# A fused attention and MLP kernel: four-sum products, casts in quarters, output banks redistributed, stores moved to ScalarE

## The chip, the cores and the metric

The kernel runs on one core of one Trainium2 chip. The metric is device time in microseconds (us). Engines are TensorE (PE), VectorE (DVE), ScalarE (ACT), GpSimd (POOL) and the synchronisation engine (SP), which in the kernel before issues every transfer. A ratio is the mean time of one kernel's fast runs over the mean of the other's fast runs in the same rounds, so it is not quite the ratio of the medians that are quoted beside it. A run is called slow when it is over 1.5% above the fastest of the same kernel; such runs count in no ratio, but the medians quoted include them.

## The reference, cut to what matters

```python
def sm_attn(qq, kk, vv):                       # softmax attention, scale 1/8
    ...
p_packed = sm_attn(p, k, v)                    # 32 packed rows per head attend to 576 keys
out = sm_attn(q, p_packed, p_packed)           # 576 queries attend to the 32 rows
x = out.transpose(0, 2, 1, 3).reshape(4608, 512)
h = x @ w_in                                   # 512 -> 2048
g = h * (1.0 / (1.0 + np.exp(-beta * h)))
return g @ w_out                               # 2048 -> 512
```

Eight batches, eight heads, 576 tokens of 64 per head. In a batch, 512 tokens are two units of output work of 256 tokens; the remaining 64 tokens of four batches together make one more unit. That is 18 units. The last product, `g @ w_out`, is done for nearly all units as a 2x2 block product with seven instead of eight block multiplications.

## The kernel before: the parts that the change and the argument touch

The program is ordered by a planner in the kernel itself. It holds tasks with an estimated duration, dependencies and a rank; it simulates the engines and emits each engine's instructions in the order that it finds. The real chip then keeps that order on each engine, whatever the real times are.

```python
LAND_US = 2.0                                  # assumed from the end of an issue to the landing
...
def plan_loads(self, b):                       # per batch: k, v, q; fp32 staging, two buffers
    ...
    m0 = m1 = self.task(None, "SP", 3.1, lambda m=main: m(0, 8), last, turn)
    ...
    c0 = self.task(("cast", b, x, 0), "POOL", 1.95, lambda f=piece: f(0, 8, "POOL"), [m0] + old, rank + 3)
...
        if b >= PE_BATCHES:                    # from batch 2 on kT and qT are made by a transfer
            d = self.task(("tr", b, x, 0), "SP", 3.0, lambda x=x: transpose_dma(x), ...)
...
self.op = pool("op", 2)                        # two output staging buffers o_sb
self.ps_h = pool("ps_h", 2, space=PSUM)
self.ps_o = pool("ps_o", 3, space=PSUM)
self.ps_a = pool("ps_a", 3, space=PSUM)
...
def sums(i):                                   # three VectorE instructions, up to 128 x 2048
    if i == 0: nc.vector.tensor_tensor(S[:, 0:2], g[:, 0:2], g[:, 2:4], ALU.add)
    elif i == 1: nc.vector.tensor_tensor(S[:, 2], g[:, 0], g[:, 3], ALU.add)
    else: nc.vector.tensor_tensor(g[:, 1:3], g[:, 1:3], g[:, 0:4:3], ALU.subtract)
...
# five takes of 512 columns from PSUM to o_sb; the first waits for the store of the unit before last
t = self.task(("take", unit, i), "DVE" if i else "ACT", 0.7 if i else 0.64, ...
              + ([("store", back)] if back and i == 0 else []), ...)
self.task(("store", unit), "SP", 1.5, lambda: self.store(unit), [t], -10)
```

(Dots and shortened calls are cuts.) The whole kernel:

The softmax here doesn't subtract the row's maximum and nothing guards it: scores larger than these inputs give would overflow.

## Time and profile before

| | before |
|---|---|
| median of three runs | 261.63 us |
| span of the profiled run | 259.1 us |
| granted TensorE clock, mean | 0.998 |
| TensorE, VectorE, ScalarE, GpSimd busy | 241.7, 199.2, 176.1, 63.4 us |

The page gives a busy time per engine, tenths of it over 40 slices, and groups of instructions; the trace behind it gives each instruction with what ended the idle time before it. On TensorE the printed end of a matmul is modelled, so its work has to be counted from the distances between starts. The prediction below shows the lines and reads them.

### The profile page before, as it was taken

The page shows a single profiled execution, that of the slowest core. Times are in us where ns is not written, and L with a number is a line of the kernel's source. Part 1 is how long each engine was busy: PE and PEld are TensorE (multiplying, and loading weights), DVE is VectorE, ACT ScalarE, POOL GpSimd, SP SyncE. Part 2 cuts the span into 40 slices and gives each one's busy share as a digit, 9 for nine tenths or more (in the row PEclk, how much of TensorE's full clock was granted, in tenths as well). Part 3 has the DMA queues.
Part 4 walks back from the last instruction along what each step waited for, and adds up shares of the span by engine and source line. Part 5 has one row for each costly group of instructions (what it writes and reads, how often), then busy time and mean ns, then how long its engine had stood idle before and what let it go on. Part 6 is the DMA issues. An engine that isn't in the chain of part 4 may idle for free.

```text
span 259.1 us, 6793 instructions
## 1 busy us (share of the span) xinstructions
PE 241.7 (93%) x2897; PEld 193.8 (75%) x2897; DVE 199.2 (77%) x288; ACT 176.1 (68%) x308; POOL 63.4 (24%) x58
## 2 busy tenths in 40 slices
PE   4899689899989999998999999999999999999990
PEld 4897576566554878886778877877889778889880
DVE  6476766887985987796888968979996688665771
ACT  1153579867877878879786987886898768765000
POOL 4320433151440741342315231600900000000000
PEclk9999999999999999999999999999999999999999
DMA  7999999997998998996998999989660102201113
GB/s 225 352 320 268 280 325 384 348 330 183 288 199 237 292 246 235 212 333 148 265 251 263 143 318 291 205 227 272 174 172 7 79 0 83 82 27 60 81 81 81
DMA packets 73471, 54.18 MB, mean 209 GB/s; under 512 B 42065, under 2 KB 66657, under 8 KB 73441
## 3 DMA queue, kind: packets, MB, share of 16 engines
q1 hardware_dynamic: 73440, 53.76, 75.2%
q8 instruction: 22, 0.36, 0.6%
q14 instruction: 9, 0.07, 0.1%
HBM read 37.23 MB, written 9.44 MB: 180 GB/s over the span
## 4 chain that ended last, share of the span: by engine, by line
PE 56%; DMA 20%; SPq 10%; ACT 4%; issue 3%; POOL 3%; DVE 2%; POOLq 0%
PE o_ps L194 31%; PE h_ps L194 14%; DMA k<-in_k_dram 9%; SPq L336 5%; DMA v<-in_v_dram 4%; PE w_ps L194 3%; DMA qT<-q_bf 3%; SPq L250 2%; PE hr_ps L194 2%; DMA q32r<-in_q_dram 2%; DMA v32r<-in_v_dram 2%; PE z_ps L194 2%; PE s_ps L194 1%; SPq L242 1%; ACT g_main L639 1%
## 5 line engine op out<-in xcount | busy, mean ns | idle before, releaser
L639 ACT ACTIVATE g_main<-h_ps 128x512 bf16<-128x512 f32 x128 | 71.1, 596 | 29.5 <-PE h_ps L194 28.6
L194 PE MATMUL h_ps<-A2T,W_bf 128*128 128x256 bf16 x512 | 70.2, 273 | 0.6 <-ACT g_main L639 0.6
L194 PEld LDWEIGHTS <-W_bf 128*128 128x128 bf16 x768 | 57.1, 98 | 12.7 <-issue 4.7
L194 PE MATMUL o_ps<-w_mix,g_main 128*128 128x256 bf16 x448 | 59.5, 273 | 0.0
L194 PEld LDWEIGHTS <-g_main 128*128 128x128 bf16 x512 | 48.2, 98 | 12.5 <-issue 2.9
L600 DVE TENSOR_TENSOR W_bf<-w_ps,beta_bc 128x512 bf16<-128x512 f32 x64 | 41.5, 682 | 5.7 <-PE w_ps L194 5.2
L194 PEld LDWEIGHTS <-g_sums 128*128 128x128 bf16 x384 | 36.4, 98 | 5.5 <-issue 1.4
L209 ACT ACT_TABLE_LOAD x28 | 35.9, 1283 | 1.2 <-PEq L1067 0.7
L194 PE MATMUL o_ps<-w_out_bf,g_sums 128*128 128x256 bf16 x256 | 33.9, 273 | 0.0
L707 DVE TENSOR_TENSOR g_sums<-g_main 128x2048 bf16<-128x2048 bf16 x14 | 21.8, 1555 | 4.8 <-ACT g_main L639 4.8
L194 PE MATMUL warm_ps<-identr 128*128 128x128 bf16 x256 | 21.9, 237 | 3.7 <-DVE bones L858 3.7
L276 POOL CAST q_bf<-q 128x2048 bf16<-128x2048 f32 (+1 forms) x7 | 14.6, 2081 | 33.5 <-DMA q<-in_q_dram 19.9
L194 PEld LDWEIGHTS <-identr 128*128 128x128 bf16 x256 | 18.0, 108 | 5.5 <-DVE bones L858 3.7
L276 POOL CAST v_bf<-v 128x2048 bf16<-128x2048 f32 (+1 forms) x7 | 13.4, 1912 | 26.2 <-PE h_ps L194 9.8
L774 DVE TENSOR_TENSOR o_sb<-o_sb,o_ps 128x512 f32<-128x512 f32 x16 | 11.0, 685 | 10.0 <-ACT g_main L639 2.5
L541 DVE TENSOR_TENSOR A2T<-E2T,rz 128x512 bf16<-128x512 bf16 (+1 forms) x24 | 13.6, 587 | 5.5 <-ACT rz L536 5.5
L276 POOL CAST k_bf<-k 128x2048 bf16<-128x2048 f32 (+1 forms) x7 | 12.4, 1771 | 21.4 <-DMA k<-in_k_dram 10.4
L711 DVE TENSOR_TENSOR g_main<-g_main 128x2048 bf16<-128x2048 bf16 x14 | 17.4, 1244 | 0.0
L194 PE MATMUL o_ps<-w_mix,g_sums 128*128 128x256 bf16 x128 | 17.3, 273 | 0.0
L194 PE MATMUL o_ps<-w_out_bf,g_main 128*128 128x512 bf16 x64 | 17.0, 380 | 0.0
L772 ACT COPY o_sb<-o_ps 128x512 f32<-128x512 f32 x16 | 9.4, 588 | 10.3 <-PE o_ps L194 10.2
L194 PEld LDWEIGHTS <-pp 64*32 64x32 bf16 x384 | 6.0, 88 | 13.5 <-issue 10.9
(86 smaller groups left out, 296.5 us busy)
## 6 DMA issues: line engine op xcount, KB each, us to landing
out_dram<-o_sb SPq DMA_DIRECT2D x16, 512.0 KB, 3.9
k<-in_k_dram SPq DMA_DIRECT2D x7, 1024.0 KB, 8.5
v<-in_v_dram SPq DMA_DIRECT2D x7, 1024.0 KB, 6.8
q<-in_q_dram SPq DMA_DIRECT2D x7, 1024.0 KB, 6.7
w_in<-in_moe_w_in_dram SPq DMA_DIRECT2D x4, 1024.0 KB, 9.4
w_out<-in_moe_w_out_dram SPq DMA_DIRECT2D x4, 1024.0 KB, 12.4
k<-in_k_dram SPq DMA_DIRECT2D x2, 512.0 KB, 5.4
k32r<-in_k_dram SPq DMA_DIRECT2D x16, 64.0 KB, 5.2
```

Of the source, the lines that this page charges most:

```text
L194: return self.nc.tensor.matmul(out, lhsT, rhs, start=start, stop=stop, tile_position=pos, skip_group_check=True)
L209: self.nc.scalar.preload_act_table_set(SETS[mode])
L250: nc.sync.dma_start(t[64 * g : 64 * g + 64, :].rearrange("p (h d) -> p h d", h=4), src[b, 4 * g : 4 * g + 4, SM:S, :].rearrange("h p d -> ...
L276: self.copy[engine](self.t[b, x][:, 0:2048].rearrange("p (t h d) -> p h t d", t=4, h=8)[:, h], self.t[b, x, "32"][:].rearrange("p (h t d) ...
L336: nc.sync.dma_start_transpose(t[:], st[b, x][:])
L541: nc.vector.tensor_tensor(part(st[b, "A2"], i), part(st[b, "E2"], i), part(st[b, "rz2"], i), ALU.mult)
L600: nc.vector.tensor_tensor(st[b, "W"][:, r, cols], st[b, "w", m][:], self.beta_bc[:, cols], ALU.mult)
L639: nc.scalar.activation(st[b, v, "g"][:, :, f, :], st[b, "h", v, f][:].rearrange("p (q n) -> p q n", q=4), AF.Silu)
L707: nc.vector.tensor_tensor(st[*unit, "S"][:, 0:2], g[:, 0:2], g[:, 2:4], ALU.add)
L711: nc.vector.tensor_tensor(g[:, 1:3], g[:, 1:3], g[:, 0:4:3], ALU.subtract)
L772: nc.scalar.copy(middle, st[*unit, "C"][:])
L774: nc.vector.tensor_tensor(ends, middle.rearrange("p (h n) -> p h n", h=2)[:, ::-1], halves(st[*unit, "D"]), ALU.subtract)
```

## The change

Its intent is to take work from VectorE and to shorten both the waits behind it and the tail. The seven products are rewritten with four sums of 128x1024 on each side (one form of instruction instead of three), and accumulate in place in two PSUM banks; takes are 256 columns wide. GpSimd casts in pieces of a quarter, so that no piece holds VectorE up for long. The softmax normalisation of the packed rows moves into pointer operands of later instructions. The PSUM banks go from h 2, o 3, att 3 to h 3, o 2, att 3. Every task gets a rank offset of its own. All stores but the last two units' are issued from ScalarE.

```diff
+STORE_US = 5.0
+STORE = 'ACT'
+RINGS = {'h': 3, 'o': 2, 'att': 3}
+OFFSETS = {0: -0.9, 1: -8.9, 2: -158.2, ...}          # 1,130 entries, cut
 def add(self, engine, us, fn, deps=(), rank=0, ...):
+    rank += OFFSETS.get(len(self.tasks), 0)
...
-    self.copy[engine](bf[:, h], f32[:, h])             # 128 x 2048
+    m = 2 if engine == "POOL" else n
+    for j in range(0, n, m):
+        self.copy[engine](to[:, j : j + m], of[:, j : j + m])   # 128 x 512
...
-    d = self.task(("tr", b, x, 0), "SP", 3.0, ...)
+    d = self.task(("tr", b, x, 0), "SP", 3.8, ...)
...
+    out, a, b, op = {0: (s[:, 0], a21, a22, ALU.add), 1: (s[:, 1], s[:, 0], a11, ALU.subtract),
+                     2: (s[:, 2], a12, s[:, 1], ALU.subtract), 3: (a21, a11, a21, ALU.subtract)}[i]
+    nc.vector.tensor_tensor(out, a, b, op)
...
+    steps = [(("g", 2), "B21", 1, True), (("g", 0), "B11", 0, True), (("S", 0), "T1", 1, True), (("S", 1), "T2", 0, False),
+             (("S", 2), "B22", 1, False), (("g", 1), "T3", 0, False), (("g", 3), "T4", 0, False)]
...
-    nc.vector.tensor_tensor(W[:, r, cols], w_ps, self.beta_bc[:, cols], ALU.mult)
+    nc.vector.scalar_tensor_tensor(W[:, r, cols], w_ps, rz1[:, r : r + 1], self.beta_bc[:, cols], ALU.mult, ALU.mult)
...
-    self.task(("store", unit), "SP", 1.5, lambda: self.store(unit), [t], -10)
+    e = STORE if len(self.outs) < 17 else "SP"
+    self.task(("store", unit), e, us, lambda: self.store(unit, e), deps, -10)
```

(The order of the first loads, of the units of the last batch and many ranks change as well.)

## The prediction

> **What bounds the kernel now.** I read the page's busy tenths first, then the stretches of 20 us, then TensorE's timeline at the two ends, then the groups by line.
>
> ```profile
> PE   4899689899989999998999999999999999999990
> ...
> ACT  1153579867877878879786987886898768765000
> ...
> PEclk9999999999999999999999999999999999999999
> DMA  7999999997998998996998999989660102201113
> ```
> The clock is never throttled, so it is no part of the story. DMA is full until about 190 us, TensorE from about 60 us on. The stretches (TensorE, its weight loads, VectorE, ScalarE, GpSimd; then clock, DMA share, GB/s) say it more sharply:
>
> ```profile
> 20.00:40.00 20.00, 16.43 (x275) 13.36 (x273) 14.41 (x26) 11.64 (x23) 5.54 (x7) 1.00 1.02 296
> ...
> 60.00:80.00 20.00, 19.18 (x208) 11.49 (x206) 16.94 (x22) 14.78 (x26) 6.04 (x5) 1.00 0.93 224
> 80.00:100.00 20.00, 20.00 (x222) 15.06 (x219) 18.05 (x24) 16.52 (x30) 8.73 (x6) 1.00 1.00 251
> ...
> 160.00:180.00 20.00, 20.00 (x263) 16.25 (x261) 17.75 (x26) 15.21 (x26) 5.52 (x4) 1.00 0.99 249
> ...
> 220.00:240.00 20.00, 20.00 (x210) 18.03 (x208) 12.36 (x17) 12.82 (x23) 0.00 (x0) 1.00 0.14 55
> ```
> From 80 us TensorE is busy 20.00 of 20. But is it streaming, or are only modelled ends joined up? In its timeline the starts of consecutive pieces give the true spacing: eight 256-column matmuls take 0.87 us, 0.109 each; sixteen 64-column hr matmuls 0.47 us (0.029 each). Counting every matmul of 80 to 120 us at such spacings gives 39.9 of 40 us, of 160 to 200 and 200 to 240 us 40, of 120 to 160 us 38.8, of 47 to 80 us 29.9 of 33. The steady state is thus a full TensorE, and the full DMA there costs it about 1 us: one late transpose at 122 us. A faster VectorE buys nothing by itself.
>
> The start is different: TensorE runs fillers on warm_ps while it waits for loads.
>
> ```profile
> 46.13 0.41 PE L194 MATMUL w_ps<-w_in_bf,pp 64*32 64x512 bf16 x8
> 46.47 0.51 PE L194 MATMUL warm_ps<-identr 128*128 128x128 bf16 x6
> 46.91 0.39 PE L194 MATMUL w_ps<-w_in_bf,pp 64*32 64x512 bf16 x1
> 47.63 0.41 PE L194 MATMUL w_ps<-w_in_bf,pp 64*32 64x512 bf16 x7 [0.33 <-DVE W_bf L600]
> ...
> 75.76 0.41 PE L194 MATMUL s_ps<-qT,pp 64*32 64x512 bf16 x8 [0.79 <-DMA qT<-q_bf]
> ```
> The last filler ends at 47 us. After it the program has 488 h, 896 output (256 columns), 64 plain output (512 columns, 0.2175 each), 256 hr, 224 w and some 420 small matmuls: 53.1 + 97.5 + 13.9 + 7.5 + 12.3 + 16.0 = 200.3 us. TensorE ends at 253.1, so 206.1 us pass: 5.8 us are holes, 3.1 of them before 80 us. The tail is 6 us:
>
> ```profile
> 252.07 1.04 PE L194 MATMUL o_ps<-w_mix,g_sums 128*128 128x256 bf16 x8
> ...
> 253.15 0.69 DVE L782 TENSOR_TENSOR o_sb<-o_sb,o_ps 128x512 f32<-128x512 f32 x1 [0.19 <-PE o_ps L194]
> 253.87 2.46 SPq L809 DMA_DIRECT2D out_dram<-o_sb  x4
> ```
> One take, four issues that need 2.46 us, and the last landing at 259.1. So span = 47 (start) + 200.3 (work) + 5.8 (holes) + 6 (tail).
>
> **What the Trainium skill says.** "SBUF — State Buffer", section "SBUF: two separate sides": VectorE and GpSimd share a port pair as an exclusive lock for a whole instruction, and a VectorE operation with two SBUF inputs contends with a GpSimd operation that reads SBUF. This trace agrees (shortest, median and longest ns of the sums' two forms):
>
> ```profile
> L707 DVE TENSOR_TENSOR g_sums<-g_main x14: 1208/1224/2914, 71.8 to 236.4; 128x2048 bf16<-128x2048 bf16 x14
> ...
> L709 DVE TENSOR_TENSOR g_sums<-g_main x14: 676/782/2374, 74.4 to 237.5; 128x1024 bf16<-128x1024 bf16 x14
> ```
> and from the groups by line:
> ```profile
> L276 POOL CAST q_bf<-q 128x2048 bf16<-128x2048 f32 (+1 forms) x7 | 14.6, 2081 | 33.5 <-DMA q<-in_q_dram 19.9
> ```
> The longest sums exceed the shortest by 1.7 us, nearly one whole GpSimd cast. "VectorE: DVE Perf Modes", the section on the TRN2 errata, gives (N+151)/0.96 ns for an fp32 tensor_tensor: 691 ns at 512, and the output takes here show 685; so I estimate 0.42 us at 256. "ScalarE: Activation LUTs", "What ACT_TABLE_LOAD costs": each 128x1 pointer operand adds about 93 ns; nothing in this trace has one, so that stays an estimate. "DMA: Bandwidth & Descriptors", "Issuing engines are not separate DMA queues": issuing from another engine saves sequencer time only. The trace cannot show that yet, but the synchronisation queue waits 55.5 us in total in front of stores (14.3 the longest) and TensorE is still full.
>
> **The change part by part.**
>
> (a) TensorE's work. The built program of the changed kernel orders 254 fillers (256 before) and, behind the last, 480 h, 952 output, 32 plain, 256 hr, 208 w, 60 z1 and the small ones: 52.2 + 103.6 + 7.0 + 7.5 + 11.4 + 17.3 = 199.0 us. Both forms have seven products of 8 matmuls at 256 columns, so the new form saves no product. One unit less is plain: 32 x 0.2175 - 56 x 0.109 = -0.9 us in all. z1 becomes ten one-column matmuls (about 0.028 each by the 64-column spacing) for ten of 128 columns (0.40 us): -0.12 per batch, -0.7 in the six batches concerned. Eight h and 16 w matmuls moved ahead of the last filler (-1.8), transposes of q and scores moved behind it (+2.1). Sum: -1.3 us.
>
> (b) VectorE. Sums: 61.2 us now; 17 units x 4 x 0.68 = 46.2. Takes: 43.9 + 2.7 now; 102 x 0.42 + 2 x 0.69 = 44.2. The 128-column reciprocal (8 x 0.952 = 7.6) becomes 2 columns, about 0.16 each: 1.3. Normalising (16 x 0.287 = 4.6) becomes one copy, 8 x 0.42 = 3.4. Mixes 6.1 to 4 x 1.22 = 4.9. W_bf, 64 x 0.682 = 41.5, gets a pointer operand: I allow 46. Sum 167.6 to 146: VectorE falls from 199 to about 178 us busy. None of it lies on TensorE's path in the steady state, so its worth is slack.
>
> (c) ScalarE. Takes 16 x 0.588 to 17 x 0.38 (-3.0), 32 exponentials with a pointer scale (+3.0), 26 table loads for 28 (-2.6); 19 store issues at about 0.5 us join its queue. About even at 68% busy.
>
> (d) GpSimd's casts in quarters. The longest lock-out of a sum falls from some 1.7 us to about 0.5, for some 0.1 us more per piece on an engine that is 24% busy.
>
> (e) PSUM. Output now accumulates in two banks; a step may start only when the take of the preceding step on its bank is done. That take costs about 0.2 (as long as takes sit idle behind the last matmul in the trace) + 0.42 + 0.1 = 0.72 us. I laid TensorE's new order out at the spacings above: of 85 such waits, 81 have at least 0.87 us of other matmuls in between, three have 0.34 to 0.43, and the very last has none (a hole of 0.7 us). About a third have under 0.95: slack only if VectorE is free. The third h bank removes the small waits for g_main (0.2 us each around 50 us).
>
> (f) Loads. The last w_in stands behind 12.2 MB in both orders, so the fillers should end at the same time, 46 to 47 us. The last w_out comes after 16.5 MB instead of 17.7, some 4 us earlier at 300 GB/s: it loosens the stretch to 80 us, where 3.1 us of holes are.
>
> (g) Tail. The last unit is now one store instead of four: saves up to 1.9 us of issue; the take shrinks by 0.27. Tail 4.5 instead of 6, plus the hole of (e).
>
> Sum: 46.5 + 199.0 + 3.5 (holes) + 0.7 + 4.5 = 254.2 us of span. The medians lie 2.5 above the span now, so 256.7; I say 256.8. The holes are my choice: fewer late transposes (they are now planned later) and smaller lock-outs, against tighter takes.
>
> **Rivals.**
> 1. The take becomes the bound. If VectorE is 0.2 to 0.4 us late at a third of the 85 waits, 28 x 0.2 to 0.4 = 6 to 11 us of holes appear in place of 3.5: 259 to 264 us. For it: the 0.15 us of slack. Against it: VectorE is 20 us lighter, and most waits have over 1 us.
> 2. Nothing moves: the order is as full as before, and holes come back elsewhere, at a late DMA or ScalarE, which now also waits for takes before it issues stores. Then only (a) and (g) remain: 258 to 260.
> 3. The start shortens too, because q's first loads no longer wait for a staging buffer and less of the early queue stalls: fillers end at 43 to 44 us, and 252 to 254 is possible. Against it: DMA is already full from 6 us, and the fillers' number is unchanged.
>
> **Range and chances.** Without any hole the floor is about 46 + 199 + 5 + 2.5 = 252.5; with rival 1 in force 262. I put 80% on 253 to 261. Faster by over 2% means below 256.4, almost my centre: 0.43; within 2% 0.51; slower 0.06, as that would need 12 us of new holes.
>
> **What would show it.** Fillers end at 46 to 47 us; VectorE busy about 178 us; sums' longest near 1.2 us instead of 2.4 to 2.9; TensorE's holes after the fillers 3 to 4 us; from the last matmul to the end about 4.5 us. I am wrong if TensorE waits for VectorE's or ScalarE's takes at o_ps for over 5 us in all (rival 1), or if the fillers end 2 us away from 47.

## The result, and the profile after

The changed kernel is correct and slower: median 272.28 us of four runs (269.0 to 273.89, two of them slow), against 262.14 of four runs of the kernel before beside it. The ratio of fast runs is 1.0304, with a 95% interval of 1.0212 to 1.0397. The profiled run is a fast one: span 267.2 us, against 259.1.

The tenths of the changed kernel's page, to be laid beside those of before:

```profile
PE   4958769898994999999999799989999999999893
...
PEclk9999979999999799999999999999999999999999
```

TensorE's row now has a 4 in the slice from about 80 to 87 us and dents later; the clock's row has a 7 twice, in the slices from 33 and from 87 us, where the row of before has nothing but 9. The stretches (TensorE, its weight loads, VectorE, ScalarE, GpSimd; clock, DMA share, GB/s) say where:

```profile
80.00:100.00 20.00, 16.50 (x183) 12.45 (x182) 14.14 (x25) 12.35 (x24) 9.57 (x17) 0.91 1.03 231
...
140.00:160.00 20.00, 18.61 (x191) 15.69 (x189) 13.59 (x26) 15.85 (x30) 3.43 (x6) 1.00 0.99 213
```

TensorE, busy 20.00 of 20 in both of these stretches in the kernel before, is idle 3.5 us in the first, where its clock averages 0.91, and 1.4 us in the second. TensorE's timeline in the changed kernel (in brackets its idle time just before, and what ended it):

```profile
35.59 0.39 PE L296 MATMUL w_ps<-w_in_bf,pp 64*32 64x512 bf16 x2 [3.40 <-POOL w_in_bf L1095]
...
49.90 0.34 PE L296 MATMUL warm_ps<-identr 128*128 128x128 bf16 x3
...
86.99 0.41 PE L296 MATMUL s_ps<-qT,pp 64*32 64x512 bf16 x8 [3.50 <-DMA qT<-q_bf]
...
89.74 1.90 PE L296 MATMUL o_ps<-w_mix,g_sums 128*128 128x256 bf16 x8
91.56 0.25 PE L296 MATMUL s2r_ps<-qT,pp 64*32 64x64 bf16 x8
...
152.06 1.08 PE L296 MATMUL h_ps<-A2T,W_bf 128*128 128x256 bf16 x8 [1.39 <-ACT g_main L756]
```

The last filler starts at 49.90 and so ends near 50, 3 us later than before. The second scores of batch 2, which began at 75.76 us, begin at 86.99, after 3.5 us of waiting for the transposed q. Right behind that wait eight output matmuls take 91.56 - 89.74 = 1.82 us instead of 0.87: the clock has halved. With the same counting as in the prediction, 199.0 us of work follow the last filler, TensorE ends at 263.1, and 263.1 - 50 - 199.0 = 14 us are holes and slow clock, against 5.8 us. The tail is 4.1 us.

Why is qT late? The chain of what released what, in the changed kernel (start, duration, what):

```profile
69.50 4.21 DMA k<-in_k_dram
73.71 0.41 POOL q_bf L399
...
74.28 12.66 DMA qT<-q_bf
```

The transfer that transposes q took 12.66 us from its issue to its landing; in the kernel before it was issued at 70.98 and landed in time for the scores at 75.76, so at most 4.8 us. The synchronisation engine's queue in the changed kernel shows its neighbours:

```profile
69.50 0.55 SPq L358 DMA_DIRECT2D k<-in_k_dram  x1
...
73.74 0.38 SPq L358 DMA_DIRECT2D v<-in_v_dram  x1
74.28 6.92 SPq L453 DMA_TRANSPOSE qT<-q_bf  x1
```

Two loads of 1 MB each stand ahead of it, that of v directly, and its issue alone took 6.92 us. In the kernel before the load of v follows qT:

```profile
70.98 2.90 SPq L336 DMA_TRANSPOSE qT<-q_bf  x1
...
79.02 0.58 SPq L242 DMA_DIRECT2D v<-in_v_dram  x1
```

And the cast of q, which has to be done first, was itself slower. GpSimd's timeline of the changed kernel, then of the kernel before:

```profile
68.38 5.33 POOL L396 CAST q_bf<-q 128x512 bf16<-128x512 f32 x4
```
```profile
67.73 1.89 POOL L276 CAST q_bf<-q 128x2048 bf16<-128x2048 f32 x1 [4.24 <-DMA q<-in_q_dram]
```

Four quarters took 5.33 us where the whole took 1.89. The trace says where the time went: one by one they took 1.68, 1.60, 1.60 and 0.61 us, and each of the first three lay beside a w_mix difference on VectorE, of two operands in SBUF. The second and third of these, in VectorE's timeline:

```profile
69.84 1.29 DVE L1135 TENSOR_TENSOR w_mix<-w_out_bf 128x2048 bf16<-128x2048 bf16 x1
...
71.39 1.29 DVE L1135 TENSOR_TENSOR w_mix<-w_out_bf,w_mix 128x2048 bf16<-128x2048 bf16 x1
```

The median quarter takes 0.61 us, so four that are left alone take some 2.5. The sums, on the other hand, did what was hoped: the longest of the first form in the changed kernel is 1.15 us (before, 2.9 for a sum twice as large and 2.4 for one of the same size).

```profile
L837 DVE TENSOR_TENSOR g_sums<-g_main x15: 674/683/1154, 58.3 to 249.7; 128x1024 bf16<-128x1024 bf16 x15
```

The second clue is the 1.39 us wait for ScalarE at 152.06. ScalarE's timeline of the changed kernel, where ACTq is its queue issuing a transfer:

```profile
151.02 0.34 ACTq L922 DMA_DIRECT2D out_dram<-o_sb  x1
151.41 2.06 ACT L756 ACTIVATE g_main<-h_ps 128x512 bf16<-128x512 f32 x4 [2.68 <-DVE o_sb L886]
```

A store stood at the head of ScalarE's queue until 151.02, as the take that it stores was not done, and everything behind it stood too. (The release that the line names, the take, was the store's; g_main does not need it.)

### The profile page after: what moved, and what is told of

Read it like the earlier page. It is cut to its first block, busy times and chain, and to the rows that moved or that the text cites. A ratio compares the mean times of both kernels' runs of the same rounds, so it can differ in the third digit from the quotient of the medians.

```text
span 267.2 us, 6970 instructions
## 1 busy us (share of the span) xinstructions
PE 242.7 (91%) x2919; PEld 196.5 (74%) x2919; DVE 179.9 (67%) x335; ACT 171.1 (64%) x307; POOL 73.9 (28%) x119
## 4 chain that ended last, share of the span: by engine, by line
PE 63%; DMA 23%; SPq 4%; DVE 4%; POOL 2%; issue 1%; ACT 1%; ACTq 0%; POOLq 0%
PE o_ps L296 37%; PE h_ps L296 16%; DMA w_in<-in_moe_w_in_dram 6%; DMA qT<-q_bf 5%; DMA q<-in_q_dram 4%; DMA w_out<-in_moe_w_out_dram 4%; PE w_ps L296 3%; PE hr_ps L296 3%; SPq L366 3%; DMA v32r<-in_v_dram 2%; DMA k<-in_k_dram 2%; PE s_ps L296 1%; PE z_ps L296 1%; PE pp_ps L296 1%; DVE W_bf L717 1%
## 5 line engine op out<-in xcount | busy, mean ns | idle before, releaser
L717 DVE SCALAR_TENSOR_TENSOR W_bf<-w_ps,rz,beta_bc 128x512 bf16<-128x512 f32 x64 | 45.6, 744 | 5.9 <-PE w_ps L296 5.9
L884 DVE TENSOR_TENSOR o_sb<-o_sb,o_ps 128x256 f32<-128x256 f32 x51 | 21.3, 418 | 29.9 <-PE o_ps L296 26.0
L296 PE MATMUL o_ps<-w_out_bf,g_main 128*128 128x256 bf16 (+1 forms) x272 | 39.9, 285 | 1.1 <-DVE w_out_bf L1110 0.9
L296 PE MATMUL o_ps<-w_mix,g_sums 128*128 128x256 bf16 x272 | 37.5, 278 | 0.6 <-DVE o_sb L886 0.6
L296 PE MATMUL o_ps<-w_mix,g_main 128*128 128x256 bf16 x240 | 32.6, 273 | 0.5 <-DVE o_sb L884 0.5
L886 DVE COPY o_sb<-o_ps 128x256 f32<-128x256 f32 x51 | 21.3, 420 | 16.9 <-PE o_ps L296 16.4
L396 POOL CAST q_bf<-q 128x512 bf16<-128x512 f32 x26 | 19.8, 799 | 40.9 <-DMA q<-in_q_dram 40.9
L396 POOL CAST k_bf<-k 128x512 bf16<-128x512 f32 x26 | 17.6, 717 | 26.8 <-DMA kT<-k_bf 11.2
L396 POOL CAST v_bf<-v 128x512 bf16<-128x512 f32 x26 | 16.6, 678 | 10.3 <-PE pp_ps L296 3.9
L296 PE MATMUL o_ps<-w_out_bf,g_sums 128*128 128x256 bf16 x136 | 18.5, 273 | 0.1
```

The lines of the kernel that those rows point to most:

```text
L296: return self.nc.tensor.matmul(out, lhsT, rhs, start=start, stop=stop, tile_position=pos, skip_group_check=True)
L396: self.copy[engine](to[:, j : j + m], of[:, j : j + m])
L717: nc.vector.scalar_tensor_tensor(st[b, "W"][:, r, cols], st[b, "w", m][:], st[b, "rz1"][:, r : r + 1], self.beta_bc[:, cols], ALU.mult, AL ...
L884: nc.vector.tensor_tensor(o, o, ps, ALU.add)
L886: self.copy[engine](o, ps)
```

## The experiments

After the result I held three theories. **A**, late arrivals: the new program makes things arrive late (qT behind v, loads and casts, a store that blocks ScalarE, an output buffer whose store has not landed), and the new form is as good as predicted. **B**, rival 1 of the prediction: takes on two output banks are too tight. **C**: a lower clock is the cause and not a consequence. All seventeen kernels gave correct results. The medians of the kernel before were 261.64 (whole casts, qT first, stores from the synchronisation engine, twice the fillers), 262.49 (third buffer, no offsets, quarters alone, three undone), 264.04 (stores from ScalarE in the kernel before, the filled hole, four undone), 263.15 (quarters, halves, split tail), 261.94 (v ahead again, two buffers again) and 262.06 (stores from ScalarE again). Six of the eleven runs of the kernel before count as slow, only because one run took 259.44; with all eleven counted three ratios, 1.0354, 1.0291 and 1.0075, would be 1.0285, 1.0225 and 1.0008.

### One suspect undone at a time

Casts whole again:

```diff
-    m = 2 if engine == "POOL" else n
+    m = n
```

> The changed kernel with GpSimd's casts whole again (128x2048 in one instruction, w_in 128x1024), every order as it was. In the changed profile the quarters cost 2.3 to 5.3 us per 2048 columns, the whole casts of before 1.89. Theory 1 (late loads and transposes, each hole over 3.4 us followed by 3.4 us at half clock): q's cast of batch 2 ends 1 to 3 us earlier, the wait for qT at 84 us falls below 3.4 us and that clock drop goes; the start's w_in casts are 0.6 us shorter. 3 to 5 us less: 266 to 269. Rival (tight takes): sums are locked out for up to 1.9 us again, takes come late, the time stays or grows by 1 to 2 us: 272 to 274.

Measured: 266.54 us, ratio 1.0157 (1.0083 to 1.0231). The second scores of batch 2 began at 82.68 with no wait for qT; GpSimd's busy time fell from 73.9 to 60.3 us. The casts in quarters are thus part of the loss, in this program.

The load of v moved behind the transpose of q, where the two are neighbours in the queue:

```diff
+    if t.engine == "SP" and t.key and t.key[0] == "load":   # hold a load of v back for one issue
+        self.held = t.fn; return
```

> The changed kernel with one thing moved: in the synchronisation queue the 1 MB load of v (batches 3 and on) stands behind the transpose of q where the two were neighbours, not ahead of it. Theory 1: 1 MB at some 300 GB/s is 3.3 us, so the 3.50 us wait for qT at 84 us falls to under 1 us and the half clock behind it (1.7 us) goes: 4 to 5 us less, 267 to 268. Rival (tight takes) and rival (only the start matters): no difference, 271 to 273.

Measured: 269.01 us, ratio 1.0162 (1.0052 to 1.0271). The scores began at 80.88 without a wait; a hole of 3.36 us for g_main appeared at 146.40, with half clock behind it.

Stores issued from the synchronisation engine, at the same place in the plan:

```diff
-    "ACT": self.nc.scalar, "SP": self.nc.sync
+    "ACT": self.nc.sync, "SP": self.nc.sync
```

> The changed kernel with every store issued by the synchronisation engine at the same place of the plan, all other orders unchanged. If stores on ScalarE hold up ScalarE (g_main waited 2.68 us behind one at 148 to 151 us, TensorE 1.39 us), that hole goes: 1 to 2 us less. But the synchronisation queue then waits for takes ahead of loads and transposes: if theory 1 holds and transposes are the weak place, they come later still, so same or up to 3 us more. Expected sum: 271 to 275.

Measured: 268.75 us, ratio 1.0163 (1.0039 to 1.0287). ScalarE's waits went, and another came up. VectorE's timeline of this run:

```profile
146.02 0.42 DVE L886 COPY o_sb<-o_ps 128x256 f32<-128x256 f32 x1 [4.27 <-DMA out_dram<-o_sb]
```

The first take of a unit waited 4.27 us for the store of the unit before last, which still occupied one of the two output buffers; TensorE waited 2.83 us behind it.

Twice as many fillers at the start:

```diff
-    self.mm(self.warm[:, 0:128], self.identr[:], self.identr[:])
+    for _ in range(2):
+        self.mm(self.warm[:, 0:128], self.identr[:], self.identr[:])
```

> The changed kernel with two filler matmuls in place of each one until 48 us of the plan, nothing else. Theory 1: the hole of 3.4 us at 32 to 35.6 us fills with fillers, the granted clock stays 1.00 in the first 50 us (now 0.5 from about 37 to 41 us). The start's end at 50 us is set by loads of w_in, so only what ran slowly behind the drop comes back: 0.5 to 1.5 us, and less spread between runs. Rival (the clock costs nothing, all is loads): no difference in time, clock 1.00 all the same.

Measured: 273.36 us, two of the four runs slow. The clock stayed 1.00 over the first 50 us, the fillers ended at 51.9, and the wait for qT grew to 5.38 us. So up to about 87 us the arrival of qT sets the time; TensorE's pace before it does not.

A third output buffer:

```diff
-    self.op = pool("op", 2)
+    self.op = pool("op", 3)
```

> The changed kernel with three output staging buffers in place of two, every order as it was. In the changed kernel the first take of a unit waits until the store of the unit before last has landed (5 us were planned, up to 8.3 measured); ScalarE and TensorE stood behind such takes near 150 us (1.39 us, in two of the experiments 2.8 and 3.4). If that is right, no wait for a take longer than 0.7 us remains there; 1 to 3 us less than the changed kernel in the same call's terms, ratio to before 1.02. The start and the wait for qT near 84 us stay. Rival (two PSUM banks are what holds the takes): no difference.

Measured: 268.47 us, ratio 1.0192 (1.0127 to 1.0257). No take waited for a store any more, but ScalarE idled for 5.43 us until an input load, q32r, landed, with its store issued right after it, and TensorE waited 4.57 us for E2T at 140.15.

No offsets per task:

```diff
-OFFSETS = {0: -0.9, 1: -8.9, ...}
+OFFSETS = {}
```

> The changed kernel with the 1,200 ranks per task taken out, so that the planner's own ranks set every order; all other parts stay. If the ranks are fitted to planned durations that the chip doesn't keep (casts in quarters, transposes, stores), the kernel without them loses little or is even as fast: 268 to 274. If they carry a real gain, it is 5 us or more slower than the changed kernel: over 277.

Measured: 271.33 us, ratio 1.0308 (1.0225 to 1.039), the same as the changed kernel. In this program the 1,130 ranks, which shape the whole order, are worth nothing that these runs can see; in the mended one below they were not taken out.

### Two parts of the change by themselves, in the kernel before

Casts in quarters alone:

```diff
-    self.copy[engine](bf[:, h], f32[:, h])
+    m = 2 if engine == "POOL" else n
+    for j in range(n * i, n * i + n, m): self.copy[engine](bf[:, j : j + m], f32[:, j : j + m])
```

> The kernel before with GpSimd's casts in quarters and nothing else. If quarters lengthen every cast by 0.5 to 1 us and more under VectorE's sums, transposes come later and the holes near 75 and 122 us grow by 1 to 2 us: 262 to 265, ratio 1.002 to 1.012. If shorter lock-outs of VectorE are worth something to TensorE: at or below before, ratio 0.99 to 1.00. The longest sum on VectorE falls from 2.9 us to below 2.0 either way.

Measured: 265.04 us, ratio 1.004 (0.9936 to 1.0143): no difference that can be told from none. In its trace TensorE's longest wait for qT is 2.73 us, where the kernel before has 1.0, so the late arrival appears here too.

Stores from ScalarE alone, all but the last two units':

```diff
-    nc.sync.dma_start(rows[:, 2 * v : 2 * v + 2, :], o[:])
+    nc.scalar.dma_start(rows[:, 2 * v : 2 * v + 2, :], o[:])
```

> The kernel before with its stores issued from ScalarE instead of the synchronisation engine, all but the last two. If a store in ScalarE's queue waits for the landing of an input load issued eight transfers earlier, ScalarE shows idle times of over 2 us that end with an input tile or an output landing, TensorE waits for g_main or E2T behind them, and the median rises to 264 to 268. If ScalarE's queue is free of that here, the time is 261 to 263, or lower, as the synchronisation engine then no longer waits for takes.

Measured: 270.77 us, ratio 1.0354 (1.0263 to 1.0446). This one change makes the kernel before as slow as the changed kernel (with all runs counted, 2.9% slower). ScalarE's timeline of this run:

```profile
124.16 0.34 ACTq L805 DMA_DIRECT2D out_dram<-o_sb  x1
124.54 0.60 ACT L639 ACTIVATE g_main<-h_ps 128x512 bf16<-128x512 f32 x1 [2.79 <-DMA k32r<-in_k_dram]
```

The idle time ends with the landing of k32r, a piece of an input, and g_main needs no k32r; the store that stood before it was issued in between. At 149.23 the same happened with qT (2.08 us). At 170.46 came the four stores of the remainder unit: ScalarE issued them for 2.93 us, had done nothing for 2.6 us ahead of that, and TensorE waited 4.67 us. In the built program of the changed kernel, 18 of ScalarE's 19 stores wait, besides VectorE, for one of eight completion counters, and the loads on the other queue wait for the same eight. The programs show the rule: a counter is reused by later transfers, on whichever queue, and each of these 18 issues waits for the very counter that it will itself increment, at the count that its former user's landing makes. In this run's program that former user is k32r for the store at 124.16 and qT for the one at 148.82, just what the trace names. On the synchronisation engine such a wait should cost little, as the loads are queued there anyway (argued, not measured); on ScalarE it holds up the activations.

### Theory C: the clock

The hole before the second scores of batch 2 filled with work of no use:

```diff
+    if b == 2 and not rest:
+        for _ in range(50): self.mm(st[b, name, 0][:, 0:128], self.identr[:], self.identr[:])
```

> The changed kernel with 50 filler matmuls (about 2.8 us) ahead of the second scores of batch 2, where TensorE waits 3.5 us for the transpose of q. The wait stays, so TensorE starts these scores at about 87 us as before; only the idle time goes. If the clock falls because TensorE is idle that long, the clock stays 1.00 between 87 and 92 us, eight output matmuls there take 0.87 us instead of 1.82, and the kernel gains about 1.6 us: 269.5 to 271. If the clock falls for another reason (a power limit, say), it falls all the same and the time stays at 271 to 273.

Measured: 269.54 us, ratio 1.0291 (1.0187 to 1.0395). The stretch from 90 us on, first in the changed kernel, then in this run (the third figure from the end is the clock):

```profile
90.00:91.00 1.00, 1.00 (x6) 0.67 (x5) 0.93 (x3) 0.00 (x0) 0.00 (x0) 0.50 1.03 303
```
```profile
90.00:92.00 2.00, 2.00 (x25) 1.50 (x24) 1.93 (x4) 1.00 (x4) 0.00 (x0) 1.00 0.98 298
```

The clock stayed at 1.00, and from the start of the scores to the first z_ps matmul 91.38 - 87.68 = 3.70 us passed instead of 92.22 - 86.99 = 5.23. So the half clock follows from TensorE's idleness, and cost 1.5 us at this place. The Trainium skill, "TensorE: Matmul & The Clock Gate", section "What's actually happening", says that one idle window of some 3.4 us on a counter that runs freely halves the clock. The traces agree in the length, as the half clock behind a hole lasts 3.4 us or twice that (88.42 to 91.84 us in the changed kernel), and the kernel before, whose longest hole after its first matmul was 1.8 us, has none. They do not show that a hole must be so long: half clock also followed holes of 2.73 us (quarters alone, 124.98) and 2.63 us (no offsets, 134.13), and did not follow one of 2.92 us (the last run with stores from ScalarE below, 146.23). Over the whole kernel the gain can't be told from none, as this run had a wait of 1.83 us for g_main at another place. Theory C falls as a first cause and stands as a surcharge on a long hole.

### All suspects undone together: the sign of one of them turns

Casts whole, qT first and three output buffers, with stores still from ScalarE (the three edits above):

> Whole casts, the transposes of q ahead of v's loads, and three output buffers together; all orders of the compute engines as in the changed kernel. If the loss is late transposes, lengthened casts and store landings, the second scores of batch 2 start at 79 to 81 us without a wait (86.99 in the changed kernel), no hole of over 1.5 us is left behind them, and with 168.0 us of counted work left plus 3 to 4 us of small holes TensorE ends at 251 to 253 and the run takes 257 to 261 us: the loss against before is gone. If the two banks and tight takes are the loss, it stays at 264 to 267.

Measured: 266.05 us, ratio 1.0107 (1.0046 to 1.0167); in the profiled run, which was its slow one, a hole of 3.05 us for ScalarE remained. The same with the stores from the synchronisation engine:

> The changed kernel with four things undone at once: GpSimd's casts whole again, the load of v behind the transpose of q, three output buffers for two, and the stores issued from the synchronisation engine. If the loss is made of these late arrivals and the form itself is as good as predicted, ScalarE no longer waits in front of g_main for the landing of an input load (4.3 and 3.1 us holes in the two earlier runs with three buffers), no hole over 2 us is left after 80 us, and the median is 259 to 262, the same as the kernel before or up to 1% faster. If the form (tighter takes on two output banks) costs time of its own, the median stays at 264 to 267 and TensorE's waits at o_ps for VectorE sum to over 3 us.

Measured: 264.0 us, ratio 1.0075 (1.0005 to 1.0145). No hole over 2 us is left after 80 us, but it is not faster than the kernel before. Of my two sentences the second came true, at its edge: TensorE's waits at o_ps for VectorE's takes sum to 3.8 us (1.4 in the changed kernel). What remains is theory B, in a form that I had not thought of. VectorE's timeline of this run, then TensorE's:

```profile
85.69 2.26 DVE L854 TENSOR_TENSOR g_sums<-g_main,g_sums 128x1024 bf16<-128x1024 bf16 x1
87.87 0.41 DVE L901 TENSOR_TENSOR o_sb<-o_sb,o_ps 128x256 f32<-128x256 f32 x1
```
```profile
88.33 1.03 PE L313 MATMUL o_ps<-w_out_bf,g_main 128*128 128x256 bf16 x8 [0.88 <-DVE o_sb L901]
```

A sum of usually 0.69 us lasted 2.26; a take stood behind it; TensorE waited for the take. The same at 155 us, where a whole cast ran from 153.98 to 155.92, the sum lasted 2.05 us and TensorE waited 1.16 us. So casts in quarters are the remedy for this form's tight takes, and had to be tried again with the other three undone; halves lie in between:

```diff
-    m = n
+    m = 2 if engine == "POOL" else n       # quarters; for halves: m = min(n, 4)
```

> The kernel of the last combined run (transpose of q first, three output buffers, stores from the synchronisation engine), but with GpSimd's casts in quarters again. In the run with whole casts two sums of VectorE lasted 2.3 and 2.0 us beside a cast, an output take stood behind each, and TensorE waited 0.9 and 1.2 us for it. If whole casts are what makes the two output banks too tight, the longest sum falls under 1.3 us, TensorE's holes for VectorE's takes before 235 us fall by about 2 us, and the median is 1 to 2 us under that run's. If the slower casts (3 us for 2 us) cost more, qT or a cast is waited for by 2 us or more and the median is 264 to 266.

> The same with casts in halves. A lock-out is at most about 1 us and a cast about 2.3 us in all. If both lock-outs and the length of a cast matter, this is the best of the three: 260 to 263, against the kernel before 0 to 1% faster. If neither matters, all three agree within 1 us.

Measured: quarters 260.14 us, ratio 0.9869 (0.9815 to 0.9923); halves 261.08 us, ratio 0.9916 (0.9859 to 0.9972). The three in order, whole, halves, quarters: 1.0075, 0.9916, 0.9869; halves and quarters cannot be told apart. The intervals exclude 1. The slow cast did not go away, it stopped mattering. GpSimd's timeline with quarters, and the queue of the synchronisation engine in the same run (its slowest of six, counted as slow, span 261.0 us):

```profile
69.91 5.33 POOL L413 CAST q_bf<-q 128x512 bf16<-128x512 f32 x4
```
```profile
75.67 3.56 SPq L470 DMA_TRANSPOSE qT<-q_bf  x1
79.27 0.59 SPq L375 DMA_DIRECT2D v<-in_v_dram  x1
```

The cast is as slow as it was and qT is issued 1.4 us later than in the changed kernel, yet with v behind it the scores began at 84.94 without a wait. The longest sum is 1.09 us, TensorE waits for no take by over 0.3 us between 65 and 240 us, and TensorE's row in this run's page is all nines from its eleventh slice to its thirty-seventh:

```profile
PE   4988749897999999999999999999999999999892
```

### Which of the three are needed

With quarters, each of the three taken back alone:

> The changed kernel with quarter casts, three output buffers and the stores from the synchronisation engine, but with v loaded ahead of the transpose of q again. If that one place in the queue matters by itself, TensorE waits 1.5 to 3.5 us for qT before the second scores of batch 2 and the kernel is 2 to 4 us slower than with all three undone (260.1): 262 to 264. If only the stores and buffers mattered, it is 260 to 261.

> The changed kernel with quarter casts, the transpose of q first and the stores from the synchronisation engine, but with two output buffers again. If the third buffer matters, the first take of some unit waits for the landing of the store two units before (as it did for 4.3 us with the stores moved alone), TensorE waits over 2 us behind it, and the time is 262 to 265. If two buffers are enough once the stores are issued from the synchronisation engine and the loads are in place, it is 259.5 to 261.5, the same as with all three undone.

> The changed kernel with quarter casts, the transpose of q first and three output buffers, but with the stores from ScalarE, as changed: the third of the three taken back. If a store in ScalarE's queue stands there until an input load issued eight transfers earlier has landed, ScalarE idles for over 2 us in front of g_main or E2T once or twice, TensorE waits behind it, and the time is 264 to 267. If the earlier loads make the stores from ScalarE harmless, it is 260 to 262, like the kernel with all three undone.

Measured: v ahead of qT again, 263.12 us, ratio 1.0004 (0.9917 to 1.0091), with a wait of 1.70 us for qT; two buffers again, 265.53 us, ratio 1.0149 (1.0067 to 1.0231); stores from ScalarE again, 265.21 us, ratio 1.0105 (1.0014 to 1.0195). VectorE's timeline with two buffers, and ScalarE's with its stores:

```profile
144.88 0.42 DVE L903 COPY o_sb<-o_ps 128x256 f32<-128x256 f32 x1 [6.11 <-DMA out_dram<-o_sb]
```
```profile
145.20 0.34 ACTq L939 DMA_DIRECT2D out_dram<-o_sb  x1
145.58 1.57 ACT L773 ACTIVATE g_main<-h_ps 128x512 bf16<-128x512 f32 x3 [4.21 <-DMA v32r<-in_v_dram]
```

TensorE waited 4.68 us behind the first and 2.92 us behind the second. With these runs all eight combinations of the three are measured, all with casts in quarters:

| stores from | qT and v | output buffers | ratio to before |
|---|---|---|---|
| ScalarE | v first | 2 | 1.0304 (the changed kernel) |
| synchronisation | v first | 2 | 1.0163 |
| ScalarE | qT first | 2 | 1.0162 |
| ScalarE | v first | 3 | 1.0192 |
| synchronisation | v first | 3 | 1.0004 |
| synchronisation | qT first | 2 | 1.0149 |
| ScalarE | qT first | 3 | 1.0105 |
| synchronisation | qT first | 3 | 0.9869 |

The mean of the four differences is 1.4% for the stores, 0.9% for the place of qT and 1.5% for the third buffer. Single differences are less sure than these, as the intervals are about 1% to either side and the rows come from several calls.

### The tail alone

Two of the last unit's four stores in the kernel before issued from ScalarE:

```diff
-    nc.sync.dma_start(self.out[lo : lo + SR, :], ...)
+    (nc.scalar if unit == ("r", 1) and e % 2 else nc.sync).dma_start(self.out[lo : lo + SR, :], ...)
```

> The kernel before with two of the last unit's four stores issued from ScalarE, which has nothing to do by then. The four issues took 2.46 us one after another at the end; in two queues they take about half. If the tail is set by these issues, the kernel gains about 1.2 us (0.5%), with the work up to the last matmul unchanged at 253 us. If ScalarE's stores wait for other transfers at the end as they do in mid-kernel, there is no gain.

Measured: 262.32 us, ratio 0.9966 (0.9912 to 1.002). In the trace both queues begin to issue at 254.16, and the longer of them needs 1.45 us instead of the 2.46 of one queue. So the issues got shorter by 1.0 us; the time agrees with a gain of that size and also with none.

## Why the prediction was right or wrong

It was wrong: 256.8 us with 253 to 261 against 272.28, and 0.06 for the outcome that came.

**Right.** The work (a) and the takes (b): VectorE is busy 179.9 us (178 said), a take of 256 columns 420 ns (0.42 us said), W_bf 45.6 us in all (46 allowed). (c)'s 93 ns for a pointer operand, an estimate from the skill, was met: the median exponential E2T took 594 ns before and 687 after. The tail (g): 4.1 us for 4.5. The lock-outs (d) shrank as said: the longest sum is 1.15 us.

**Wrong, in the terms of the sum.** I had 46.5 + 199.0 + 3.5 + 0.7 + 4.5 = 254.2. The trace has 50 + 199.0 + 14 + 4.1 = 267.1. The start is off by 3.5 us, the holes by 10; the last place in the sum gives 0.4 back. The step that failed first is the term of 3.5 us for holes, which rested on "fewer late transposes (they are now planned later)": with slow clock it came to 14 us, and its largest part is a later transpose, qT, at 3.5 us of waiting and 1.5 of half clock. Of the two signs of being wrong the second came, fillers that end at 50; of the first, takes at o_ps, there were 1.4 us.

- Step (f), the start, took the order of the bytes for the order of arrival. The fourth w_in was issued at 36.53 us behind a w_out whose buffer had to be freed by the cast of another w_in, and was cast from 46.00 on, against 44.49 before. And "it loosens the stretch to 80 us" was the opposite of what came: the second scores of batch 2 began 11.2 us later. I never asked what would be in the queue ahead of the transposes, though the built program has that order.
- Step (d) costed a quarter at "some 0.1 us per piece". A whole cast of 2048 columns took 1.8 to 2.1 us in the mean, four quarters 2.7 to 3.2, the worst 5.33. Quarters left alone add 0.14 us each (0.61 against a fourth of 1.89), so the 0.1 was near; what it left out is VectorE's turns between the quarters, which made three of them 1.6 to 1.7 us beside w_mix. I had called GpSimd idle enough at 24% busy; but the cast of q lies on the path to qT.
- Step (c) held the 19 stores in ScalarE's queue to be worth their issue time, and quoted the Trainium skill ("DMA: Bandwidth & Descriptors", "Issuing engines are not separate DMA queues") for it. What the page says of the DMA engines stands. But an issue is an instruction in order, and what it waits for, all behind it waits for too: ScalarE lost 2.7 us at one store that waited for its take in the changed kernel, 4.2 and 5.4 at stores that waited for an input's landing in two variants, and the kernel before lost 3.5% (2.9% with all runs counted) by this alone.
- "The clock is no part of the story" held for the kernel before. The two holes of 3.4 and 3.5 us cost it: 1.5 us were measured at the second.
- The output buffers I did not name at all: with two of them a take waited 4.3 and 6.1 us for a landing in two variants, where no take of the kernel before waits for one. Why the new order meets the landing is not shown.

**Slips in its arithmetic.** The 2.5 us from span to time set the profiled run's span against the median of other runs; that run itself took 260.84 us, 1.7 over its span, so 0.8 of the 256.8 was not earned. In (b), 64 x 0.682 is 43.6, while the 41.5 is the page's busy time. In (a), the difference for the plain unit has its sign turned; the saving of 0.9 us is right.

**The rivals.** Rival 2, holes that come back at a late DMA or at ScalarE waiting for takes, named the right places, but I let it go no higher than 260, and knew nothing of its waits for landings. Rival 1 did not show in the changed kernel, whose quarters keep the takes short, but it did in the run with whole casts, at 0.9 and 1.2 us a time.

**What was right about the intent.** With three small things put right, the changed kernel is 1.3% faster than the kernel before (0.8 to 1.9%), 260.14 us. I had expected 1.8%. How much of the 1.3% is due to the form is open, as the kernel before was not run with a third output buffer. A good part of the remainder is at the start: in this version's profile the fillers end at 51 us, not at 46.5, and that was not cured. One attempt at it (more fillers) showed only that TensorE's pace is not the reason; a better order of the first loads stays open.

## What to carry to other kernels

When stores move to a busy compute engine, ask what else an issue there waits for, and look in the profile for idle time of that engine that ends with the landing of a transfer that its next instruction does not need. A remedy has to be judged with the other faults removed: casts in quarters cost 1.5% in the changed program and gained 2% in the mended one (1.4% with all runs of the kernel before counted), because in the first the cast's length was on the path and in the second only its lock was. And put a small transfer that TensorE waits for ahead of a large one that nothing waits for yet.

## What the Trainium skill lacked or had wrong

- "DMA: Bandwidth & Descriptors", "Issuing engines are not separate DMA queues", speaks of sequencer time alone. Elsewhere the page has it that a wait is held by the issuing sequencer; it does not say that a store in a compute engine's queue can so stand until another queue's transfer has landed, where the program reuses completion counters: 4.21 us of ScalarE until v32r landed, and 3.5% of the kernel before by moving its stores alone. That is the program's doing, not the DMA engines', and a sentence on it would have changed the prediction.
- The same page does not say how long a transpose by DMA takes behind other loads: issued right behind a load of 1 MB, with another shortly ahead, one needed 12.66 us to land, where 4.8 us had been enough; its issue alone held the synchronisation engine's queue for 6.92 us.
- "SBUF — State Buffer", on the shared port pair: the lock agrees (a sum of 0.69 us lasted 2.26 beside a cast of 2.07). What it leaves out is the price of splitting the GpSimd instruction, as VectorE can come in before each piece: four quarters took 2.7 to 3.2 us in the mean for 1.8 to 2.1 whole, and 5.33 us beside three differences on VectorE, where four quarters left alone would take some 2.5.
- "TensorE: Matmul & The Clock Gate": the 3.4 us of half clock agree. That an idle window of 3.4 us is needed does not: half clock followed holes of 2.73 and 2.63 us, and in the changed kernel it began at 88.42 us, 1.4 us after the hole of 3.50 had ended. The page does not say how much idleness within a window is enough.
